# A convolution kernel generator on one Trainium2 core: twelve of W1's sixteen columns made in wide products, W2 of two channel halves in one tile

## The chip, the cores and the metric

The kernel runs on one NeuronCore of a Trainium2 chip. The core has a matrix engine (PE; PEld is its weight load), a vector engine (DVE), an activation engine (ACT), a general engine (POOL) and a queue engine for transfers (SP). The metric is the time of one execution in microseconds of device time, taken as the median of several runs.

## The reference: what is computed

```python
x   = u                                         # 1 x 2048 x 576
sa, ca, ga, sb, cb, gb = silu(c) @ w_mod        # six rows of 576
h   = layernorm(x) * (1 + ca) + sa
dt  = exp(log_dt);  A = -exp(log_A_real) + 1j * A_imag;  C = (C_real + 1j * C_imag) * dt
K   = 2 * Re( sum_n C[d,n] * exp(A[d,n] * dt[d] * l) )     # 576 channels, l = 0..2047, 128 modes
y   = causal_convolution(h, K) + h * D_skip                # by FFT
x   = x + ga * y
h   = layernorm(x) * (1 + cb) + sb
out = x + gb * (relu(h @ w1) @ w2)              # w1 576 x 4608, w2 4608 x 576
```

## The kernel before, in words

The program has two stages that matter here.

**Stage 1 (function `first`)** makes the convolution kernel K. The 128 modes lie on the partitions. Channels go in six passes, g = 0 to 5, of G = 96 channels, each as two halves (u = 0, 1) of H = 48. The position l is split as 512·s + 32·a + b: a tile W2 holds a mode's 32 values over b for each channel (complex), a tile W1 its 16 values over a, and PE multiplies them into K (`products`, 192 small matmuls a pass, bank `kps`). One pass does this:

- `exps(g+1)`: PE makes five phase banks (`ph`), ACT takes their exponential (tiles E).
- `turns(g+1)`: PE makes three phase banks, ACT rounds each to an integer (tile k), DVE subtracts it (k<-ph,k): the fraction of a turn.
- `sines(g+1)`: ACT takes sine and cosine of these; DVE and POOL multiply them with E into W2 (`half_values`); `start` makes W1's first column, through the tiles Tc and tc; `powers` makes the powers z^32, z^64 ... of each mode (tile Zp, in PSUM); DVE scales them (`moduli`).
- `doubling(g, i)`: W1's columns m to 2m are its columns 0 to m times a power, for m = 1, 2, 4, 8. Each is two products (t, T) and two sums. For m = 1, 2, 4 DVE does all four; for m = 8 POOL does the sums.
- `products(g)`: the first 96 matmuls of a pass (half u = 0) are issued after the doubling; those of u = 1, called `late`, are spread between the phase matmuls of the next pass.

The helpers `v`, `stt`, `pool`, `act` and `matmul` keep program order on each engine, so within `first` every engine's queue is the order in which the code is written. In the profile all of one helper's instructions have one line: L62 is a DVE product, sum or difference, L65 a DVE fused product, L68 one of POOL, L59 one of ACT, L71 a matmul.

**Between the stages** `conv(0)` runs in program order too: the first kernel tile gets its skip term (`skip`, kt<-kt, L1263), `h` is multiplied by ca and sa gets added (L641, L642); PE transforms the kernel tile and h (ps_f, L852), ACT evacuates them (tile Z), and DVE does butterflies over four tiles of 576 columns (`butterfly1`: W<-Z; `butterfly2`: U, K or V<-W). Beside this the last pass's products are evacuated (ke), stored to DRAM (kd), loaded back in another layout (kt) and transformed again; the product of spectra (Y, T) and the inverse transform follow.

**Stage 2 (function `ffn`)** runs four blocks of 512 rows. Each has 36 steps of matmuls into hps (L1332) and acc (L1358); the remaining convolution work (`rest`, `conv(1)` to `conv(3)`, `finish`) is cut into pieces by generators and put between them. A generator yields a number, its cost in the planner's units, and `step` draws pieces until a target is reached.

Of the kernel before, what the change touches and what calls it, by code (L numbers as in the profile page):

```python
# [49 lines left out]
class KGen:  # L50
# [22 lines left out]
    def open(self, ctx):  # L73
# [3 lines left out]
        self.ph, self.ps = pool("kg_ph", space=PSUM), pool("kg_ps", space=PSUM)  # L77

    def banks(self, name):
        return self.ph.tile([P, 2, 512], F32, tag="ph", bufs=2, name=name)  # L80

    def setup(self, I):
# [3 lines left out]
        kept = self.tc.keep_in_program_order  # L86
        tmp = lambda n: self.pw.tile([KR, NH, P], F32, tag="W2", bufs=5, name=n)
        lar, ai = tmp("lar"), tmp("ai")
        dtT = pc.tile([KR, NH], F32, name="dtT")
# [92 lines left out]
    def exps(self, g):  # L182

        E = self.E[g] = []
        for s0, n in ((0, 8), (8, 8), (16, 8), (24, 8), (32, 6)):
            e = self.pt.tile([P, 2, 8 * H], F32, tag="E", bufs=8, name=f"E_{g}")
            e = self.chunk(e, s0, n)
            self.act(e, self.times(g, self.zz[1], s0, n), AF.Exp)
            E.append(e)
            yield  # L190

    def turns(self, g):

        F = self.F[g] = []
        for s0, n in ((0, 8), (17, 8), (32, 6)):
# [17 lines left out]

    def half_values(self, g, W2, E, f, odd):


        nc, v, p = self.nc, self.v, self.pool
        j0 = 0 if odd else 16
        El, Eh = E
        su = self.chunk(self.banks(f"s_{g}"), 0, 8)  # L220
        c = None if odd else self.abs(f)
        self.act(su, f, AF.Sin, scale=TWO_PI)
        c = c if c is not None else self.abs(f)
        self.cos(c, c)
        n = 8 if odd else 7
        ends = self.start(g, su[:, :, :, 7], c[:, :, :, 7]) if odd else ()
        hi, lo = slice(j0 + 8, j0 + 16), slice(j0, j0 + n)
        for u in range(2):
            v(W2[u][:, 1, :, hi], su[:, u], Eh[:, u], ALU.mult)
            self.stt(  # L230
                W2[u][:, 1, :, lo][:, :, ::-1], su[:, u, :, 0:n], -1.0,
                El[:, u, :, 0:n][:, :, ::-1], op0=ALU.mult, op1=ALU.mult,
            )
        for u in range(2):
            p(W2[u][:, 0, :, hi], c[:, u], Eh[:, u], op=ALU.mult)
            p(
                W2[u][:, 0, :, lo][:, :, ::-1], c[:, u, :, 0:n], El[:, u, :, 0:n][:, :, ::-1],
                op=ALU.mult,
            )
            if not odd:  # L240
                nc.gpsimd.tensor_copy(W2[u][:, 0, :, 23], El[:, u, :, 7])
                nc.gpsimd.memset(W2[u][:, 1, :, 23], 0.0)
        return ends
# [18 lines left out]
    def powers(self, g, e, f):  # L262

        Z = self.ps.tile([P, 2, 512], F32, tag="Z", name=f"Zp_{g}")[:, :, 0 : 4 * G]
# [4 lines left out]
        self.act(by_u(Z[:, 1]), f[:, :, 0:4], AF.Sin, scale=-TWO_PI)  # L269
        self.act(by_u(zs[:, :, 1]), f[:, :, 4:6], AF.Sin, scale=-TWO_PI)  # L270
        self.cos(by_u(Z[:, 0]), c[:, :, 0:4])
        self.cos(by_u(zs[:, :, 0]), c[:, :, 4:6])
        for r in (1, 0):
            self.pool(by_u(zs[:, :, r]), by_u(zs[:, :, r]), e[:, :, 4:6], op=ALU.mult)
        self.Z[g] = Z, zs

        def moduli():
            for r in (1, 0):
                self.v(by_u(Z[:, r]), by_u(Z[:, r]), e[:, :, 0:4], ALU.mult)

        return moduli

    def doubling(self, g, i, u):

        v, p = self.v, self.pool
        Z = self.Z[g][0]
        m, n = 1 << i, (u.stop - u.start) * H
        W1 = self.W1[g][:, :, u].rearrange("p r u c a -> p r (u c) a")
        X, out = W1[:, :, :, 0:m], W1[:, :, :, m : 2 * m]
        zr, zi = (  # L290
            Z[:, r, i, u.start * H : u.stop * H].unsqueeze(1).unsqueeze(3)
            .broadcast_to([P, 2, n, m])
            for r in range(2)
        )
        if m == 8:
            t = self.pc.tile([P, 16 * H], F32, tag="T0", bufs=2, name="T0")
            T = self.pc.tile([P, 16 * H], F32, tag="T1", bufs=2, name="T1")
        else:
            t = self.pc.tile([P, 8 * H], F32, tag="t", bufs=2, name="t")[:, : 2 * n * m]
            T = self.ps.tile([P, 512], F32, tag="T", name="T")[:, : 2 * n * m]  # L300
        t, T = (x.rearrange("p (r c a) -> p r c a", r=2, c=n) for x in (t, T))
        v(t, X, zr, ALU.mult)
        v(T, X, zi, ALU.mult)
        yield
        add = p if m == 8 else v
        add(out[:, 0], t[:, 0], T[:, 1], op=ALU.subtract)
        add(out[:, 1], t[:, 1], T[:, 0], op=ALU.add)

# [15 lines left out]
    def first(self, setup, mod):  # L324
# [8 lines left out]
        def sines(g):  # L333
            E, F = self.E.pop(g), self.F.pop(g)
            W2 = W2s[g] = [
                self.pw.tile([P, 2, H, 32], F32, tag="W2", bufs=5, name=f"W2_{2 * g + u}")
                for u in range(2)
            ]
            ends = self.half_values(g, W2, E[2:4], F[0], True)
# [4 lines left out]
            for u in range(2):  # L344
                nc.sync.dma_start(out=k.W2d[2 * g + u], in_=W2[u].rearrange("p r c b -> p (r c b)"))
            self.moduli = self.powers(g, E[4], F[2])
# [48 lines left out]
        for g in range(NG):  # L395
            self.moduli()
            if g + 1 == NG:
                next(early)
            double = [
                self.doubling(g, i, u)  # L400
                for i, u in (
                    (0, slice(0, 2)), (1, slice(0, 2)), (2, slice(0, 1)), (2, slice(1, 2)),
                    (3, slice(0, 1)), (3, slice(1, 2)),
                )
            ]
            if g + 1 < NG:
                for i, _ in enumerate(self.exps(g + 1)):
                    some(late, 2 - i % 2)
            run(*double[:2])
            next(mod, None)  # L410
            run(double[2])
            if 0 < g < 5:
                next(early)
            if g + 1 < NG:
                turns = self.turns(g + 1)
                for _ in range(2):
                    next(turns)
                    some(late, 2)
                next(double[3])
                next(turns)  # L420
                run(late, turns, double[3])
            else:
                run(late, double[3])
# [11 lines left out]
            )  # L435
            a, late = (self.products(ps[g], self.W1[g], W2s[g][u], u) for u in range(2))
            if g + 2 == NG:
                self.kt0 = self.pw.tile([P, 16, 72], F32, tag="W2", bufs=5, name="kt_0")
                k.load_kt(self.kt0, 0, 0, nc.sync)
# [132 lines left out]
class Body:  # L572
# [34 lines left out]
    def early(self, kg):  # L607
# [23 lines left out]
        ))  # L631
        self.h0 = h = kg.pw.tile([P, 4, D], F32, tag="W2", bufs=5, name="h_0")
        for i in (0, 2, 1, 3):
# [5 lines left out]
        kept(self.skip(self.kt0, 0, nc.vector))  # L639
        for i in (0, 2, 1, 3):  # L640
            kept(nc.vector.tensor_tensor(h[:, i], h[:, i], self.m["ca"], op=ALU.mult))  # L641
            kept(nc.vector.tensor_tensor(h[:, i], h[:, i], self.m["sa"], op=ALU.add))  # L642
        self.wm = {}
        for nm in ("sb", "cb"):
            self.wm[nm] = kg.pw.tile([P, 5, D], F32, tag="W2", bufs=5, name=f"wm_{nm}")
        yield
# [14 lines left out]
    def mod(self, kg):  # L661
# [7 lines left out]
        names = (  # L669
            (2, "ga", kg.pc, "W1", 2), (1, "ca", kg.pc, "W1", 2), (0, "sa", kg.pw, "W2", 5)  # L670
        )
# [191 lines left out]
    def butterfly1(self, Z, W):  # L863
        v = self.vec.tensor_tensor
        for i in range(2):
            v(W[:, 2 * i], Z[:, i], Z[:, i + 2], op=ALU.add)
            v(W[:, 2 * i + 1], Z[:, i], Z[:, i + 2], op=ALU.subtract)
            yield 1.5

    def butterfly2(self, W, X, sgn):  # L870
# [4 lines left out]
        yield 1.5  # L875
        i, j = (1, 3) if sgn < 0 else (3, 1)
        v(X[:, i, 0], B[:, 0], Dd[:, 1], op=ALU.add)
        v(X[:, i, 1], B[:, 1], Dd[:, 0], op=ALU.subtract)
        v(X[:, j, 0], B[:, 0], Dd[:, 1], op=ALU.subtract)
        v(X[:, j, 1], B[:, 1], Dd[:, 0], op=ALU.add)  # L880
        yield 1.8

# [681 lines left out]
```

## Time and profile before

| | us |
|---|---|
| median of three runs | 1333.97 (1328.8 to 1339.76) |
| the profiled execution | 1333.12 |
| its span, first to last instruction | 1331.4 |
| mean granted PE clock | 0.945 of full |

The profile is of one execution. Its parts are a page of busy shares, a chain of what ended last (followed back from the end, each step put down to what released it), groups of equal instructions, and a list of instructions in order of time. In such a list a row has the start, the duration, the engine, the line, the operation, out<-in with shapes, the count that was merged, and in square brackets how long the engine stood idle before it and who ended that. A row of the chain has the start, the length, the engine and tile.

### The profile page before, as it was taken

The page shows a single profiled execution, that of the slowest core. Times are in us where ns is not written, and L with a number is a line of the kernel's source. Part 1 is how long each engine was busy: PE and PEld are TensorE (multiplying, and loading weights), DVE is VectorE, ACT ScalarE, POOL GpSimd, SP SyncE. Part 2 cuts the span into 40 slices and gives each one's busy share as a digit, 9 for nine tenths or more (in the row PEclk, how much of TensorE's full clock was granted, in tenths as well). Part 3 has the DMA queues.
Part 4 walks back from the last instruction along what each step waited for, and adds up shares of the span by engine and source line. Part 5 has one row for each costly group of instructions (what it writes and reads, how often), then busy time and mean ns, then how long its engine had stood idle before and what let it go on. Part 6 is the DMA issues. An engine that isn't in the chain of part 4 may idle for free.

```text
span 1331.4 us, 25993 instructions
## 1 busy us (share of the span) xinstructions
PE 1209.0 (91%) x10720; PEld 956.7 (72%) x10720; DVE 895.4 (67%) x1324; ACT 494.5 (37%) x863; POOL 162.8 (12%) x260
## 2 busy tenths in 40 slices
PE   4566676989989999999999999999999999999997
PEld 3344554667767687777777887887888888888885
DVE  5989988999986999689468993558995231111112
ACT  5678623222223422622243225433223453232321
POOL 0756502011000100100001000100000000000000
PEclk9557788999999999999999999999999999999999
DMA  8557982989878967799879985868996557666651
GB/s 272 214 221 296 304 307 84 350 296 331 307 253 304 337 224 277 247 402 342 281 276 338 357 321 156 288 203 305 346 363 198 175 181 223 198 198 202 192 168 54
DMA packets 122379, 345.85 MB, mean 260 GB/s; under 512 B 23916, under 2 KB 24212, under 8 KB 111508
## 3 DMA queue, kind: packets, MB, share of 16 engines
q1 hardware_dynamic: 105364, 226.96, 51.2%
q0 software_dynamic: 16384, 115.85, 23.1%
q8 instruction: 84, 1.38, 0.4%
q10 hardware_dynamic: 512, 1.38, 0.3%
q14 instruction: 35, 0.29, 0.1%
HBM read 262.73 MB, written 81.40 MB: 258 GB/s over the span
## 4 chain that ended last, share of the span: by engine, by line
PE 68%; DVE 17%; DMA 7%; issue 4%; ACT 2%; POOL 1%; SPq 0%; ACTq 0%; DVEq 0%; POOLq 0%
PE acc L1358 28%; PE hps L1332 27%; PE ps_f L852 5%; DMA L1d<-w 3%; PE kps L71 2%; PE ph L71 2%; DVE T L482 2%; DVE W1r L484 2%; PE ps_i L1059 2%; PE kps L517 1%; DVE w L1302 1%; DVE W1r L486 1%; DVE W1r L488 1%; DVE w L1314 1%; DVE T L62 1%
## 5 line engine op out<-in xcount | busy, mean ns | idle before, releaser
L1332 PE MATMUL hps<-xh,w 128*128 128x512 f32 x1152 | 395.2, 403 | 1.2 <-ACT xh L47 1.2
L1358 PE MATMUL acc<-w,hh 128*128 128x512 f32 x1152 | 366.4, 400 | 3.3 <-ACT hh L1337 3.2
L1338 DVE SCALAR_TENSOR_TENSOR hl<-hps,hh 128x512 fp32r<-128x512 f32 x144 | 99.0, 687 | 311.5 <-ACT hh L1337 310.8
L1332 PEld LDWEIGHTS hps<-xh,w 128*128 128x128 f32 x1152 | 217.8, 190 | 49.7 <-ACT xh L47 2.5
L1358 PEld LDWEIGHTS acc<-w,hh 128*128 128x128 f32 x1152 | 215.1, 188 | 50.6 <-ACT hh L1337 4.1
L1332 PE MATMUL hps<-xl,w 128*128 128x512 f32 x576 | 228.5, 397 | 0.7 <-DVE xl L47 0.5
L1358 PE MATMUL acc<-w,hl 128*128 128x512 f32 x576 | 223.1, 399 | 1.8 <-DVE hl L1338 1.8
L1337 ACT ACTIVATE hh<-hps 128x512 fp32r<-128x512 f32 x144 | 86.0, 597 | 327.7 <-PE hps L1332 320.5
L1307 ACT ACTIVATE w<-r 128x576 fp32r<-128x576 f32 x141 | 96.7, 686 | 216.5 <-PE acc L1358 216.1
L1332 PEld LDWEIGHTS hps<-xl,w 128*128 128x128 f32 x576 | 109.4, 190 | 24.7 <-DVE xl L47 1.7
L1358 PEld LDWEIGHTS acc<-w,hl 128*128 128x128 f32 x576 | 107.7, 189 | 26.1 <-DVE hl L1338 3.7
L1297 ACT ACTIVATE w<-r 128x640 fp32r<-128x640 f32 x140 | 102.6, 733 | 59.1 <-DMA L1d<-w 53.8
L1332 PE MATMUL hps<-xs,w 128*128 128x512 f32 x288 | 97.8, 409 | 0.0
L71 PE MATMUL kps<-W,W 128*32 128x16 f32 x2304 | 39.6, 210 | 47.3 <-POOL W L68 28.4
L1038 DVE TENSOR_TENSOR Y<-Y,T 128x1152 f32<-128x1152 f32 x60 | 79.3, 1349 | 0.0
L71 PEld LDWEIGHTS kps<-W,W 128*32 128x32 f32 x2304 | 34.8, 143 | 60.7 <-POOL W L68 31.0
L853 ACT ACTIVATE Z<-ps_f 128x288 f32<-128x288 f32 x120 | 49.0, 410 | 70.5 <-PE ps_f L852 68.5
L517 PEld LDWEIGHTS kps<-W1r,W2r 128*32 128x32 f32 x3456 | 45.2, 113 | 38.4 <-issue 19.7
L517 PE MATMUL kps<-W1r,W2r 128*32 128x48 f32 (+2 forms) x3456 | 52.5, 202 | 15.6 <-ACT ker L527 9.4
L1478 POOL DMA_DIRECT2D out_dram<-x x16 | 8.7, 545 | 466.9 <-DVE x L1470 464.5
L1332 PEld LDWEIGHTS hps<-xs,w 128*128 128x128 f32 x288 | 53.2, 188 | 11.1
L1358 PE MATMUL acc<-hh,w 128*128 128x512 f32 x144 | 57.5, 399 | 0.0
(235 smaller groups left out, 1574.5 us busy)
## 6 DMA issues: line engine op xcount, KB each, us to landing
r<-in_w_dram SPq DMA_DIRECT2D x144, 320.0 KB, 6.0
r<-in_w_dram SPq DMA_DIRECT2D x144, 288.0 KB, 3.9
w<-L1d SPq DMA_DIRECT2D x108, 320.0 KB, 4.1
w<-L2d SPq DMA_DIRECT2D x108, 288.0 KB, 2.8
W2r<-W2d POOLq DMA_DIRECT2D x18, 1536.0 KB, 9.4
W2d<-W SPq DMA_DIRECT2D x12, 1536.0 KB, 8.6
Ua<-Ud POOLq DMA_DIRECT2D x15, 1152.0 KB, 9.5
W<-W1d POOLq DMA_DIRECT2D x18, 768.0 KB, 9.6
```

Source lines behind the costliest of these rows:

```text
L71: self.tc.keep_in_program_order(self.nc.tensor.matmul(*args, **kw))
L482: v(T, X, zi, op=ALU.mult)
L517: nc.tensor.matmul(ps[32 * dd : 32 * dd + 32, q, :], W2[:, r, ch], W1[:, r, ch], start=(r == 0), stop=(r == 1),)
L852: nc.tensor.matmul(o, fc[:, n2, c, :], src(n2), start=True, stop=True)
L853: ev = nc.scalar.activation(Z[:, n2, c], ps[:, :PC], AF.Copy)
L1038: v(y, y, T, op=op or ALU.add)
L1297: copy(g - 1)(w1[g][:, 0], r1[g], AF.Copy)
L1307: copy(g)(w[:, 0:D], r2[g], AF.Copy)
L1332: nc.tensor.matmul(ps, a, x, start=(i == 0), stop=(i == 13))
L1337: nc.scalar.activation(hh, ps, AF.Relu)
L1338: nc.vector.scalar_tensor_tensor(hl, ps, 0.0, hh, op0=ALU.max, op1=ALU.subtract)
L1358: nc.tensor.matmul(acc[i], a, x, start=(f == 0 and seen[i] == 1), stop=(f == NF - 1 and seen[i] == (3 if i < 4 else 2)),)
```

## The change

Four edits:

1. The table of powers gets 384 beside 128 and 256. W1's columns 4 to 15 are made at once: columns 0 to 3 times z^128, z^256 and z^384 (`quarters`), as two products of 1152 columns for the real and two for the imaginary part on DVE, and one sum of 1152 columns each on POOL. The doublings for m = 4 and m = 8 go. Zp, the last E, the last k grow from 6 to 7 powers.
2. W2 of both halves lies in one tile (`pair`, two buffers). The sine product with the upper columns, and all of POOL's cosine products, take both halves in one instruction.
3. `h` and one weight tile share such a pair in the last pass; h is multiplied in four instructions of 1152 columns.
4. The butterflies take two tiles in one instruction (1152 columns, or 576 where there were 288), with other planner costs (1.35 for 1.5, 1.5 for 1.8).

```diff
-POWERS = (32, 64, 128, 256, 512, 1024)
+POWERS = (32, 64, 128, 256, 384, 512, 1024)
+    def pair(self, name):
+        return self.pw.tile([P, 2, 2, H, 32], F32, tag="W2", bufs=2, name=name)
...
     def half_values(self, g, W2, E, f, odd):
+        v(W2[:, :, 1, :, hi], su, Eh, ALU.mult)
         for u in range(2):
-            v(W2[u][:, 1, :, hi], su[:, u], Eh[:, u], ALU.mult)
             self.stt(
...
-        for u in range(2):
-            p(W2[u][:, 0, :, hi], c[:, u], Eh[:, u], op=ALU.mult)
...
+        p(W2[:, :, 0, :, hi], c, Eh, op=ALU.mult)
...
+    def quarters(self, g):
+        v, p = self.v, self.pool
+        W1 = self.W1[g].rearrange("p r u c a -> p r (u c) a")
+        shape = [P, G, 3, 4]
+        X = [W1[:, r, :, 0:4].unsqueeze(2).broadcast_to(shape) for r in range(2)]
+        out = [W1[:, r, :, 4:16].rearrange("p c (j a) -> p c j a", j=3) for r in range(2)]
+        zr, zi = (
+            self.Z[g][0][:, r, 2:NP].rearrange("p j c -> p c j").unsqueeze(3).broadcast_to(shape)
+            for r in range(2)
+        )
+        for r, op in ((0, ALU.subtract), (1, ALU.add)):
+            T = self.pc.tile([P, 12 * G], F32, tag="T0", bufs=2, name="T0")
+            T = T.rearrange("p (c j a) -> p c j a", j=3, a=4)
+            v(out[r], X[r], zr, ALU.mult)
+            if r:
+                yield
+            v(T, X[1 - r], zi, ALU.mult)
+            p(out[r], out[r], T, op=op)
+            yield
...
     def first(self, setup, mod):
-            run(*double[:2])
+            self.doubling(g, 0)
+            self.doubling(g, 1)
             next(mod, None)
-            run(double[2])
+            next(quarters)
...
-                next(double[3])
+                next(quarters)
                 next(turns)
-                run(late, turns, double[3])
+                run(late, quarters, turns)
...
-            run(*double[4:])
...
     def butterfly1(self, Z, W):
-        for i in range(2):
-            v(W[:, 2 * i], Z[:, i], Z[:, i + 2], op=ALU.add)
-            v(W[:, 2 * i + 1], Z[:, i], Z[:, i + 2], op=ALU.subtract)
-            yield 1.5
+        for i, op in enumerate((ALU.add, ALU.subtract)):
+            v(W[:, i::2], Z[:, 0:2], Z[:, 2:4], op=op)
+            yield 1.35
```

How this moves DVE's queue inside a pass: the rows of pass 2 from its statistics (BN_AGGR) to the first product of the next pass's sines (Tc). First before; the three k rows are the subtractions of `turns`, the T rows with 768 columns the products for m = 8, the t and T rows with 384 those for m = 4:

```order
L624 BN_AGGR mv_289<-st_1196 128x2
L62 TENSOR_TENSOR k_1200<-ph_1201,k_1200 128x768
L62 TENSOR_TENSOR t<-W_2_1041,Zp_1075 128x384
L62 TENSOR_TENSOR T<-W_2_1041,Zp_1075 128x384
L62 TENSOR_TENSOR k_1222<-ph_1223,k_1222 128x768
L62 TENSOR_TENSOR k_1248<-ph_1249,k_1248 128x2x288
L62 TENSOR_TENSOR W_2_1041<-t,T 128x48x4 x2
L62 TENSOR_TENSOR T_1257<-W_2_1041,Zp_1075 128x768
L62 TENSOR_TENSOR T_1258<-W_2_1041,Zp_1075 128x768
L62 TENSOR_TENSOR T_1263<-W_2_1041,Zp_1075 128x768
L62 TENSOR_TENSOR T_1264<-W_2_1041,Zp_1075 128x768
L62 TENSOR_TENSOR Tc<-cc,s_1370 128x192
```

And of the changed kernel, the same stretch of the same pass:

```order
L633 BN_AGGR mv_288<-st_1134 128x2
L63 TENSOR_TENSOR k_1138<-ph_1139,k_1138 128x768
L63 TENSOR_TENSOR W_2_989<-W_2_989,Zp_1015 128x96x12
L63 TENSOR_TENSOR k_1160<-ph_1161,k_1160 128x768
L63 TENSOR_TENSOR T_1181<-W_2_989,Zp_1015 128x1152
L63 TENSOR_TENSOR k_1184<-ph_1185,k_1184 128x2x336
L63 TENSOR_TENSOR Tc<-cc,s_1293 128x192
```

The third subtraction stood ahead of two sums and four products; now it stands right ahead of Tc. The first two wide products stand ahead of BN_AGGR.

On POOL, the same pass, with the semaphores each row waits for. Before: W_4 and W_5 are the two W2 tiles of the next pass, W_1 is this pass's W1 with its four sums for m = 8:

```order
L242 MEMSET W_4_1034 128x48
L241 COPY W_4_1034<-E_755 128x48 [waits Activation_49]
L68 TENSOR_TENSOR W_1_707<-T_923,T_924 128x48x8 [waits DMAHW5_49,DMAHW4_49,DVE_49]
L68 TENSOR_TENSOR W_1_707<-T_923,T_924 128x48x8
L68 TENSOR_TENSOR W_1_707<-T_929,T_930 128x48x8 [waits DVE_49]
L68 TENSOR_TENSOR W_1_707<-T_929,T_930 128x48x8
L68 TENSOR_TENSOR tc<-cc,c 128x192 [waits Activation_49,Pool_49]
```

Of the changed kernel, where W_2_983 is the next pass's pair and W_1_680 this pass's W1:

```order
L246 COPY W_2_983<-E_720 128x2x48 [waits DMAHW1_49,PE_49,DMAHW3_49,Activation_49,Pool_49]
L247 MEMSET W_2_983 128x2x48
L69 TENSOR_TENSOR W_1_680<-W_1_680,T_821 128x96x12 [waits DMAHW5_49,DMAHW4_49,DVE_49]
L69 TENSOR_TENSOR W_1_680<-W_1_680,T_872 128x96x12 [waits DVE_49]
L69 TENSOR_TENSOR tc<-cc,c 128x192 [waits Activation_49,Pool_49]
```

Two sums took the place of four, and the copy ahead of them now waits for PE and for two transfers as well: the pair was used by the pass before, whose `late` products and stores must be done.

On DVE in the last pass, from the doubling for m = 2 to the first butterfly. Before (kt is the skip term, m_gb the tile that holds it until then; t and T are buffers, numbered by use):

```order
L62 TENSOR_TENSOR W1_5_2048<-t_2110,T_2111 128x96x2 x2
L62 TENSOR_TENSOR t_2116<-W1_5_2048,Zp_5_2082 128x384
L62 TENSOR_TENSOR T_2117<-W1_5_2048,Zp_5_2082 128x384
L62 TENSOR_TENSOR W1_5_2048<-t_2116,T_2117 128x48x4 x2
L62 TENSOR_TENSOR t_2218<-W1_5_2048,Zp_5_2082 128x384
L62 TENSOR_TENSOR T_2219<-W1_5_2048,Zp_5_2082 128x384
L62 TENSOR_TENSOR W1_5_2048<-t_2218,T_2219 128x48x4 x2
L1263 TENSOR_TENSOR kt_0_1943<-kt_0_1943,m_gb_213 1x4x72
```

Of the changed kernel:

```order
L63 TENSOR_TENSOR W1_5_1921<-t_1975,T_1976 128x96x2 x2
L63 TENSOR_TENSOR W1_5_1921<-W1_5_1921,Zp_5_1947 128x96x12
L63 TENSOR_TENSOR T0_1981<-W1_5_1921,Zp_5_1947 128x1152
L63 TENSOR_TENSOR W1_5_1921<-W1_5_1921,Zp_5_1947 128x96x12
L63 TENSOR_TENSOR T0_2081<-W1_5_1921,Zp_5_1947 128x1152
L1272 TENSOR_TENSOR kt_0_1817<-kt_0_1817,m_gb_213 1x4x72
```

The skip term had only the products and sums for m = 4 ahead of it, and those for m = 8 came after h; now all four wide products stand ahead of it.

More of the change, by code (lines that the diff above doesn't have):

```diff
@@ L86, in setup @@
         kept = self.tc.keep_in_program_order
-        tmp = lambda n: self.pw.tile([KR, NH, P], F32, tag="W2", bufs=5, name=n)
-        lar, ai = tmp("lar"), tmp("ai")
+        both = self.pair("lar_ai")[:KR].rearrange("p u r c b -> p u (r c b)")
+        lar, ai = (
+            both[:, i, 0 : NH * P].rearrange("p (h n) -> p h n", n=P) for i in range(2)
+        )
         dtT = pc.tile([KR, NH], F32, name="dtT")
@@ L334, in sines @@
             E, F = self.E.pop(g), self.F.pop(g)
[L335 to L338, printed above, removed]
+            W2 = W2s[g] = self.pair(f"W2_{g}")
             ends = self.half_values(g, W2, E[2:4], F[0], True)
@@ L435, in first @@
             )
-            a, late = (self.products(ps[g], self.W1[g], W2s[g][u], u) for u in range(2))
+            a, late = (self.products(ps[g], self.W1[g], W2s[g][:, u], u) for u in range(2))
             if g + 2 == NG:
-                self.kt0 = self.pw.tile([P, 16, 72], F32, tag="W2", bufs=5, name="kt_0")
+                self.kt0 = self.pw.tile([P, 16, 72], F32, tag="WX", bufs=1, name="kt_0")
                 k.load_kt(self.kt0, 0, 0, nc.sync)
```

105 lines of the change are left out of this document (47 added, 58 removed).

## The prediction

> **What bounds the kernel now.** I read the busy time of stretches first (us; busy time and count of PE, PEld, DVE, ACT, POOL; then granted clock, DMA share, GB/s).
>
> ```profile
> 700.00:800.00 100.00, 100.00 (x436) 81.12 (x434) 91.53 (x104) 31.42 (x55) 7.57 (x13) 1.00 0.92 337
> 1000.00:1100.00 100.00, 100.00 (x452) 81.91 (x452) 39.38 (x71) 42.06 (x71) 2.18 (x4) 1.00 0.62 186
> ```
>
> In stage 2 PE is busy all the time, whether DVE works 91.5 or 39.4 us of 100: DVE time saved there, such as the wide butterflies of `conv(1)` to `conv(3)`, ends nothing earlier. What counts is when stage 2 starts. In stage 1 I first read the PE list: the rows in which `products` of passes 1 to 4 start in earnest.
>
> ```profile
> 75.42 2.22 PE L71 MATMUL kps<-W,W 128*32 128x16 f32 x148 [0.67 <-POOL W L68]
> ...
> 97.32 2.80 PE L71 MATMUL kps<-W,W 128*32 128x16 f32 x190 [0.68 <-POOL W L68]
> ...
> 115.74 2.80 PE L71 MATMUL kps<-W,W 128*32 128x16 f32 x190 [0.68 <-POOL W L68]
> ...
> 135.30 3.11 PE L71 MATMUL kps<-W,W 128*32 128x16 f32 x223 [0.67 <-POOL W L68]
> ```
>
> These passes take 21.90, 18.42 and 19.56 us; the one before, from pass 0 to 1, I take as like the first of them. Next, DVE's list of two of them: the 18.4 us pass without a wait, and the first subtraction of the 21.9 us one.
>
> ```profile
> 89.40 0.96 DVE L62 TENSOR_TENSOR k<-ph,k 128x768 f32<-128x768 f32 x1 [3.17 <-ACT k L59]
> ...
> 108.03 0.90 DVE L62 TENSOR_TENSOR k<-ph,k 128x768 f32<-128x768 f32 x1
> 108.85 0.54 DVE L62 TENSOR_TENSOR t<-W,Zp 128x384 f32<-128x384 f32 x1
> 109.31 0.55 DVE L62 TENSOR_TENSOR T<-W,Zp 128x384 f32<-128x384 f32 x1
> 109.78 1.61 DVE L62 TENSOR_TENSOR k<-ph,k 128x768 f32<-128x768 f32 x2
> 111.31 0.60 DVE L62 TENSOR_TENSOR W<-t,T 128x192 f32<-128x192 f32 x2
> 111.83 3.54 DVE L62 TENSOR_TENSOR T<-W,Zp 128x768 f32<-128x768 f32 x4
> 115.29 0.35 DVE L62 TENSOR_TENSOR Tc<-cc,s 128x192 f32<-128x192 f32 x1
> ```
>
> The fast pass is bound by DVE. The slow one is bound by a loop: POOL's sums, PE's products, the phase matmuls, ACT, DVE (3.17 us idle), POOL. So a DVE saving counts in full only in the fast pass, and there only if DVE doesn't start to wait.
>
> **What the change costs, part by part.** DVE's instructions follow each other at 0.46 us for 384 columns (108.85 to 109.31) and 0.865 for 768 (3.46 us for four, 111.83 to 115.29); so 384 more columns cost 0.405, and 1152 take 1.27. Out per pass: two m = 4 halves, each 0.93 (108.85 to 109.78) and 0.52 (111.31 to 111.83), 2.9 together, and four m = 8 products, 3.46. In: four products of 1152, 5.08. That is -1.28. The joined sine products save 2 x 0.055 = -0.11; moduli 2 x 96 columns longer, +0.2; a subtraction longer by 96, +0.1. **Net -1.1 us of DVE a pass.**
>
> But the third subtraction moves from ahead of 4 us of products to right ahead of Tc, which needs ACT's cosine. ACT's list shows the third rounding and the first cosine; an evacuation, a table load, a sine and an absolute value lie between:
>
> ```profile
> 109.61 0.65 ACT L59 ACTIVATE k<-ph 128x576 int32<-128x576 f32 x1 [1.37 <-PE ph L71]
> ...
> 113.57 0.94 ACT L59 ACTIVATE c<-c,halfpi 128x768 f32<-128x768 f32 x1
> ```
>
> The third rounding follows DVE's first subtraction (its phase matmul needs that bank), and the cosine ends at 114.51: 5.6 us after the first subtraction ends (108.93). Before, DVE had 6.36 us to do in that time (108.93 to 115.29), so nothing waited. Now it has a wide product, a subtraction, a wide product and a subtraction: 1.27 + 0.87 + 1.27 + 0.77 = 4.2. **DVE waits 1.5 us for ACT where it saved 1.1: a DVE-bound pass gets 0.4 longer, 18.8.** Queued behind the waiting Tc are the pass's sines, moduli and doublings; POOL's cosine products wait for the same cosine anyway.
>
> In a PE-bound pass the wait is free, and what counts is from the first subtraction to POOL's last sum. POOL's price for 1152 columns is not in the trace; its forms are:
>
> ```profile
> L68 POOL TENSOR_TENSOR W<-T,T 128x384 f32<-128x384 f32 x24 | 24.5, 1055 | 42.4 <-DVE T L62 35.1 <-issue 7.3
> ...
> L68 POOL TENSOR_TENSOR zs<-zs,E 128x192 f32<-128x192 f32 x12 | 7.0, 608 | 0.0
> ```
>
> By the slope from 192 to 384 (447 ns) it is 1.055 + 4 x 0.447 = 2.84; three separate ones bound it above at 3.2; a smaller slope, 2.5, below. I take 2.7, as the 192 row is of another tile. In the 21.9 us pass: first subtraction at 89.40 as before, then 0.87, 1.27, 0.87, 1.27, and the last product ends at 93.7. POOL's first sum now stands behind a copy that waits for `late` on PE, which ends where the last phase matmul starts:
>
> ```profile
> 90.64 0.79 PE ph L71 x2
> ```
>
> So sums 91.1 to 93.8 and 93.8 to 96.5; before, 97.3: **-0.8** (between -1.2 and +0.2 by the bounds). Two such passes, one of 18.8 for 18.4 and one near 18.8 for 19.6 (the DVE-bound length): `products` of pass 4 start 1.6 - 0.4 + 0.8 = 2.0 us earlier, at 133.3.
>
> Then comes the last pass and what hangs on it. Chain and DVE list:
>
> ```profile
> 140.43 0.18 DVE L628 RECIPROCAL mv<-mv 128x4 f32<-128x4 f32 x1 [0.17 <-ACT mv L626]
> ...
> 144.77 0.55 DVE L62 TENSOR_TENSOR t<-W,Zp 128x384 f32<-128x384 f32 x1
> ...
> 147.96 0.44 DVE L1263 TENSOR_TENSOR kt<-kt,m_gb 1x288 f32<-1x288 f32 x1
> ...
> 157.61 4.65 DVE L47 TENSOR_TENSOR W<-Z 128x576 f32<-128x576 f32 x4
> ...
> 165.00 2.75 DVE L47 TENSOR_TENSOR W<-Z 128x576 f32<-128x576 f32 x4
> ```
>
> The next Tc keeps its place, half a us ahead of `products` (115.29 to 115.74 before; now 5.7 and 6.2 after the first subtraction), so it is 2.0 earlier too. The reciprocal waits for ACT's root (0.17), and the root follows the sines on ACT, not DVE; as Tc now starts at its cosine and no longer 0.8 after it, the reciprocal comes later against Tc by about 0.7: 2.0 - 0.7 = 1.3 earlier than before. Between it and the skip term stood 3.19 us of m = 4 (144.77 to 147.96); now four wide products, 5.1: +1.9. **The skip term comes 0.6 later.** From there the chain of waits runs through PE's transforms, the last products, two transfers of the kernel tile and its second transform to the butterfly of the last row:
>
> ```profile
> 148.61 13.37 PE ps_f L852 x48
> ...
> 163.73 6.02 issue
> ...
> 195.99 0.23 DVE K L47
> ```
>
> All of it moves by +0.6. The joined h products (8 of 576 at 0.67 by the slope to 4 x 1.27, -0.3) and the three wide butterflies from 157 on (2 x 1.27 and 4 x 0.67 is 5.2 each, where 6 x 0.67 and 4 x 0.36 is 5.5 and the first lost 1.9 more, 4.65 to 2.75) are hidden by it; without that cover they would give 0.3 + 0.9 + 1.9 = 3.1. That a first wide butterfly needs all eight evacuations and not four is hidden likewise. After 195.99 one and a half butterflies save 0.4. Stage 2 starts 0.2 later, and **1333.1 + 0.2 = 1333.3**; the median shown is 0.85 above its profiled run, so I say 1334.
>
> **A rule against it.** When POOL's sums of the last pass ran beside butterflies, four W<-Z took 4.65 us (157.61) and alone 2.75 (165.00). The Trainium skill, SBUF — State Buffer, section "Who interferes with whom", says that a DVE instruction with two SBUF inputs and a GpSimd instruction that reads SBUF contend for one shared port pair, an exclusive lock. The trace agrees that they slow each other. Now the skip term, with two such inputs, follows the last product just as the first wide sum ends and the second starts; caught behind one, it and all after it come up to 2.7 us later.
>
> **Rivals.**
> - *The saving comes through* (0.2): ACT is ready earlier than I think, or the chain at 148 isn't what counts. Five passes of -1.1, +1.9 at the skip term and -0.4: 1329. With DVE the bound to the end, the sixth pass's -1.3 and the hidden 3.1 in place of the +1.9: -10.3, 1323. Say 1327. For it: no DVE wait in the pass at 108. Against: the 5.6 us.
> - *The wide products run slower than contiguous ones* (0.1, the other side). Their columns come in runs of four, three powers apart in PSUM. The t row of m = 1, runs of one, took 0.477, where 0.55 for 384 (109.31) less 0.20 would be 0.35:
>
> ```profile
> L62 DVE TENSOR_TENSOR t<-W,Zp 128x192 f32<-128x192 f32 x6 | 2.9, 477 | 0.2
> ```
>
>   127 ns per 192 is 0.76 per wide product. Two of four are off the path in each pass (under the wait, or under PE), two on it: 5 x 1.52 + 4 x 0.76 = 10.6, so 1344. It decides from about 1.4 us a product. Against: rows with runs of two and four (0.46 for 384) show no such price.
> - *POOL becomes the bound* (0.1): sums of 3.7, a sixth over my upper bound, make three passes +1.2 in place of -0.8 (90.64 + 0.5 + 7.4 is 98.5), +6; or the skip term is caught, +2.7. 1336 to 1342, say 1340.
> - *The pauses without a releaser on PE* (6.02 at 163.73, and smaller) shift (0.1): plus or minus 5.
>
> **How the numbers follow.** Forecast 0.5, 1329 to 1339, predicted time 1334. The range 1325 to 1342 takes in most of the first rival and of the third. About 1% (13 us) is what a measurement of this kernel tells from no change: faster by more needs all savings and a lost pause, 0.04; slower by more needs the slow products and a second mishap, 0.06; the rest 0.9.
>
> **What would show it.** In the changed profile: wide products of 1.27 to 1.35 us; Tc idle 1 to 2 us for ACT's cosine in each pass; `products` of pass 4 at 132 to 135; skip term at 147 to 150; stage 2's first hps row at 223 to 228. I am wrong if Tc starts without a wait, if POOL's sums exceed 3.2 us, or if stage 2 starts outside those bounds.

## The result, and the profile after

| | before | after |
|---|---|---|
| median of seven runs, us | 1329.86 (1328.67 to 1339.76) | 1344.68 (1340.73 to 1350.7) |
| the profiled execution | 1333.12 | 1342.17 |
| its span | 1331.4 | 1340.3 |
| mean granted PE clock | 0.945 | 0.94 |

The ratio on record, to which this document keeps, is 1.0085 with a 95% interval of 1.0061 to 1.0110 (the two medians alone would give 1.011): the changed kernel is slower by 0.85%. That is inside "within 1%", where the prediction had put 0.9. But the forecast was no change (1334), and 1344.68 lies 2.7 us above the range's upper end.

Where did the time go? ACT makes one `hh` in each of the 144 steps of stage 2, so these rows serve as milestones. Each kernel's list at step 22, in block 0, and at the last step, first before, then after:

```profile
432.67 0.59 ACT L1337 ACTIVATE hh<-hps 128x512 fp32r<-128x512 f32 x1
...
1314.29 0.60 ACT L1337 ACTIVATE hh<-hps 128x512 fp32r<-128x512 f32 x1 [5.75 <-PE hps L1332]
```

```profile
432.65 0.59 ACT L1346 ACTIVATE hh<-hps 128x512 fp32r<-128x512 f32 x1
...
1323.24 0.60 ACT L1346 ACTIVATE hh<-hps 128x512 fp32r<-128x512 f32 x1 [5.75 <-PE hps L1341]
```

At step 22 the two kernels are level, after all of stage 1. All 9 us are lost behind it, in the stage that the prediction called covered. By the same rows the lateness is 5.82 at step 42, 7.68 at step 90 and 8.95 at the last; what follows accounts for the 5.8 up to step 42. The busy times of four stretches of the changed kernel (columns as in the prediction) show where PE stopped being busy:

```profile
455.00:500.00 45.00, 42.06 (x177) 32.38 (x176) 43.45 (x51) 14.61 (x26) 3.19 (x6) 0.99 0.70 247
500.00:545.00 45.00, 39.58 (x160) 30.30 (x160) 42.41 (x71) 11.02 (x20) 1.05 (x2) 0.97 0.69 243
700.00:800.00 100.00, 100.00 (x434) 80.70 (x433) 87.31 (x87) 31.60 (x56) 8.08 (x14) 1.00 0.94 350
1000.00:1100.00 100.00, 100.00 (x448) 81.62 (x447) 40.54 (x63) 39.15 (x65) 0.00 (x0) 1.00 0.63 185
```

And two of them before:

```profile
455.00:500.00 45.00, 44.71 (x192) 35.02 (x192) 43.86 (x63) 15.18 (x27) 3.30 (x7) 1.00 0.76 260
500.00:545.00 45.00, 41.93 (x174) 32.72 (x173) 41.30 (x73) 14.19 (x27) 0.95 (x2) 0.96 0.78 277
```

The stretches at 700 and 1000, the only ones that the prediction read, are as full as they were. From 455 to 545 PE was not always busy before either (86.64 of 90 us), and there it loses 5.0 more. DVE is busy for 43 of 45 us: it is the bound here. The chain of waits of before had said so, in three of its pieces:

```profile
469.24 2.54 DVE T L1036 x2
471.78 2.54 DVE Y L1038 x2
...
500.42 10.30 DMA Ua<-Ud
```

What DVE waits for stands in its list. Before, `conv(1)` forms K from the tiles Z. Half of its `butterfly1` starts at 430.72, half of a later `butterfly1` at 450.69, and then comes the product with Ua, which POOL has loaded from DRAM:

```profile
430.72 0.74 DVE L866 TENSOR_TENSOR W<-Z 128x576 f32<-128x576 f32 x1
...
450.69 0.76 DVE L866 TENSOR_TENSOR W<-Z 128x576 f32<-128x576 f32 x1
451.36 0.75 DVE L867 TENSOR_TENSOR W<-Z 128x576 f32<-128x576 f32 x1
...
453.50 2.62 DVE L1036 TENSOR_TENSOR T<-K,Ua 128x1152 f32<-128x1152 f32 x2
```

After:

```profile
435.45 2.63 DVE L876 TENSOR_TENSOR W<-Z 128x1152 f32<-128x1152 f32 x2 [0.73 <-ACT Z L863]
...
456.55 1.36 DVE L1045 TENSOR_TENSOR T<-K,Ua 128x1152 f32<-128x1152 f32 x1 [4.44 <-DMA Ua<-Ud]
457.83 2.62 DVE L876 TENSOR_TENSOR W<-Z 128x1152 f32<-128x1152 f32 x2
```

Three things changed. The first wide butterfly starts at 435.45, when ACT has evacuated the last Z, where half of it ran at 430.72. So K is saved 1.0 us later and the load of Ua issued 0.7 later (POOL's list, before and after):

```profile
440.01 0.55 POOL L843 DMA_DIRECT2D Rd<-K  x1 [3.54 <-DVE K L880]
...
446.06 0.54 POOL L839 DMA_DIRECT2D Ua<-Ud  x1 [2.85 <-DMA Rd<-K]
```

```profile
441.05 0.55 POOL L853 DMA_DIRECT2D Rd<-K  x1 [4.61 <-DVE K L889]
...
446.73 0.53 POOL L849 DMA_DIRECT2D Ua<-Ud  x1 [2.35 <-DMA Rd<-K]
```

The load itself took longer, too: 9.8 us from issue to landing, where it took 7.4 before. That is the larger part of Ua's lateness, and why it did is not shown. And the half butterfly that filled DVE's time until Ua landed (450.69) is now part of a wide one, which needs Z tiles that are not there yet (ACT starts on the last at 455.23) and stands behind the product with Ua (457.83). DVE idles 4.44 us, and there is no slack behind it. PE then waits for what DVE makes:

```profile
488.44 1.21 PE L1068 MATMUL ps_i<-V,gc 128*128 128x288 f32 x4 [1.04 <-DVE V L882]
...
497.28 1.24 PE L1068 MATMUL ps_i<-V,gc 128*128 128x288 f32 x4 [1.20 <-DVE x L1073]
```

In stage 1, the rows in which `products` of passes 1 to 4 start, and the transform behind the skip term, from PE's list of after:

```profile
75.01 2.21 PE L72 MATMUL kps<-W,W 128*32 128x16 f32 x148 [2.31 <-POOL W L69]
...
95.98 2.80 PE L72 MATMUL kps<-W,W 128*32 128x16 f32 x190 [2.30 <-POOL W L69]
...
115.87 2.80 PE L72 MATMUL kps<-W,W 128*32 128x16 f32 x190 [2.31 <-POOL W L69]
...
135.22 3.23 PE L72 MATMUL kps<-W,W 128*32 128x16 f32 x225 [2.33 <-POOL W L69]
...
151.53 5.64 PE L862 MATMUL ps_f<-kt,fcK 128*128 128x288 f32 x16 [5.33 <-issue]
```

Pass 4 comes 0.08 us earlier (135.30 before), not 2.0. The transform comes 2.9 us later (148.61 before). By the first hps row 0.94 of that is left (225.76 for 224.82), and by step 22 nothing.

### The profile page after: what moved, and what is told of

It is laid out like the page before. It is cut to its first block, busy times and chain, and to the rows that moved or that the text cites. A ratio compares the mean times of both kernels' runs of the same rounds, so it can differ in the third digit from the quotient of the medians.

```text
span 1340.3 us, 25783 instructions
## 1 busy us (share of the span) xinstructions
PE 1216.0 (91%) x10720; PEld 960.2 (72%) x10720; DVE 882.2 (66%) x1168; ACT 497.9 (37%) x863; POOL 166.8 (12%) x212
## 4 chain that ended last, share of the span: by engine, by line
PE 64%; DVE 18%; DMA 9%; issue 5%; ACT 2%; POOL 2%; SPq 0%; POOLq 0%; ACTq 0%; DVEq 0%
PE hps L1341 25%; PE acc L1367 24%; PE ps_f L862 4%; DMA Ua<-Ud 4%; PE kps L526 3%; DVE T L1045 3%; DVE Y L1047 3%; PE kps L72 2%; DMA L1d<-w 2%; PE ph L72 2%; DVE W L876 1%; POOL W L69 1%; PE ps_i L1068 1%; DMA r<-in_w_dram 1%; DVE T L491 1%
```

## The experiments

All ratios are to the kernel before on the same chip. Lateness is against the profile before, at step 0, 22, 42 and the last step; each is of one execution, so its start in stage 2 is good to a few us only (the runs of one kernel spread over some 10 us). The last column, what a kernel loses from step 22 to 42, is what separates them. What is lost after step 42 does not: 3.1 us in the changed kernel, but also 2.0 in e1, 3.5 in e9 and 0.0 in e11, all with the old butterflies; its cause stays open.

| kernel | ratio | 95% | late at 0 | 22 | 42 | end | 22 to 42 |
|---|---|---|---|---|---|---|---|
| changed | 1.0085 | 1.0061 to 1.0110 | 0.95 | -0.02 | 5.82 | 8.95 | 5.8 |
| e1, old butterflies | 1.0039 | 1.0021 to 1.0057 | 2.04 | -1.57 | -1.12 | 0.84 | 0.4 |
| e2, edit 4 alone | 1.0070 | 1.0045 to 1.0095 | 0.96 | -1.09 | 5.23 | 9.91 | 6.3 |
| e3, wide, old costs | 1.0061 | 1.0040 to 1.0082 | 1.68 | 1.32 | 4.79 | 6.03 | 3.5 |
| e4, first butterfly in halves | 1.0053 | 1.0034 to 1.0071 | 5.47 | 4.18 | 3.64 | 5.10 | -0.5 |
| e5, skip term first | 1.0026 | 1.0006 to 1.0047 | 6.38 | 6.13 | 5.75 | 6.15 | -0.4 |
| e6, sums early | 0.9994 | 0.9969 to 1.0018 | 4.32 | 3.62 | 3.23 | 6.65 | -0.4 |
| e7, edit 1 alone | 1.0000 | 0.9979 to 1.0022 | -0.54 | -0.69 | -0.83 | 1.35 | -0.1 |
| e8, new costs alone | 1.0011 | 0.9989 to 1.0033 | 4.87 | 2.29 | 5.71 | 7.91 | 3.4 |
| e9, stores by POOL | 1.0008 | 0.9991 to 1.0025 | -0.91 | -2.48 | -2.69 | 0.85 | -0.2 |
| e10, products at once | 1.0079 | 1.0054 to 1.0104 | 11.01 | 9.96 | 9.57 | 11.68 | -0.4 |
| e11, edits 2 and 3 alone | 1.0004 | 0.9990 to 1.0019 | 1.83 | 0.28 | 0.28 | 0.32 | 0.0 |
| e12, all orders | 1.0008 | 0.9988 to 1.0029 | -0.45 | -2.01 | -2.46 | -0.84 | -0.4 |

### The butterflies: e1 to e4, and e8

**e1** is the changed kernel with the butterflies and costs of before.

```diff
-        for i, op in enumerate((ALU.add, ALU.subtract)):
-            v(W[:, i::2], Z[:, 0:2], Z[:, 2:4], op=op)
-            yield 1.35
+        for i in range(2):
+            v(W[:, 2 * i], Z[:, i], Z[:, i + 2], op=ALU.add)
+            v(W[:, 2 * i + 1], Z[:, i], Z[:, i + 2], op=ALU.subtract)
+            yield 1.5
```

> The changed kernel with the old butterflies: two tiles a yield, 576 and 288 columns, old planner costs. Edits 1 to 3 stay. Theory A (the wide butterflies cost the time, in stage 2, since a wide one starts only when all eight evacuations are there, and DVE has no slack between 430 and 540 us): level with before, 1327 to 1335, and the lateness of stage 2's steps against before is under 1.5 us after step 42, where the changed kernel has 5.8. Theory B (the new stage 1 shifts the transfers, and the loss in stage 2 follows from that): as the changed kernel, 1340 to 1346.

It measured 1.0039 and loses 0.4 us from step 22 to 42 where the changed kernel loses 5.8. **e2** is the counterpart, the kernel before with edit 4 alone:

```diff
-            v(W[:, 2 * i], Z[:, i], Z[:, i + 2], op=ALU.add)
-            v(W[:, 2 * i + 1], Z[:, i], Z[:, i + 2], op=ALU.subtract)
-            yield 1.5
+            v(W[:, i::2], Z[:, 0:2], Z[:, 2:4], op=op)
+            yield 1.35
...
-        yield 1.8
+        yield 1.5
```

> The kernel before with only the wide butterflies and their new planner costs (edit 4 alone). Theory A: slower by about 8 us, 1336 to 1342, with PE waiting for DVE near 490 to 530 us. Theory B: level with before or up to 3 us faster, since stage 1 is as before.

1.0070: most of the loss, with stage 1's code untouched. DVE's list has the wait for Ua:

```profile
456.23 1.36 DVE L1035 TENSOR_TENSOR T<-K,Ua 128x1152 f32<-128x1152 f32 x1 [5.18 <-DMA Ua<-Ud]
```

Edit 4 has two parts. **e3** keeps the wide instructions and gives the planner the old costs:

```diff
-            yield 1.35
+            yield 1.5
...
-        yield 1.5
+        yield 1.8
```

> The changed kernel with the wide butterflies, but the planner's costs of before (1.5 and 1.8 in place of 1.35 and 1.5). Theory A1 (the form costs the time: its start waits for all eight evacuations): no change against the changed kernel, 1340 to 1346. Theory A2 (the lower costs cost it, because the planner puts more work into a step than DVE can do): most of the 9 us come back, 1329 to 1336.

It measured 1.0061 and loses 3.5 us from step 22 to 42. **e8** is the kernel before with the new costs and no other change:

```diff
-            yield 1.5
+            yield 1.35
...
-        yield 1.8
+        yield 1.5
```

> The kernel before with only the planner's costs of the butterflies lowered (1.35 and 1.5 for 1.5 and 1.8), the instructions as before. By the traces of the changed kernel, e2 and e3, stage 2 loses 8 to 9 us with wide butterflies and new costs, 4.3 with wide butterflies and old costs. Theory A1 (the form is what costs, through the late start): at most 2 us slower, 1330 to 1334. Theory A2 (the costs alone shift work and PE waits for DVE): 4 us slower or more, 1335 to 1339.

Its trace loses 3.4 us in the same place, as PE's busy time from 500 on shows (41.93 before):

```profile
500.00:545.00 45.00, 40.11 (x159) 30.62 (x158) 42.25 (x75) 10.77 (x20) 1.05 (x2) 0.92 0.69 243
```

There the lower costs put more products ahead of what PE needs from DVE: a weight tile w starts at 520.95, behind four T and Y instructions in a row from 515.87 on, and PE waits for it as it does not before:

```profile
521.22 0.79 PE L1358 MATMUL acc<-hh,w 128*128 128x512 f32 x1 [1.31 <-DVE w L1313]
```

The changed kernel waits 1.98 us at the same row (521.21); e3, with the old costs, has no such wait and loses its time earlier, at 489 to 499 us. The time of e8, 1.0011, is not told apart from no change. **e4** has the first butterfly in halves, the second wide, and the old cost for the first:

```diff
-        for i, op in enumerate((ALU.add, ALU.subtract)):
-            v(W[:, i::2], Z[:, 0:2], Z[:, 2:4], op=op)
-            yield 1.35
+        for i in range(2):
+            v(W[:, 2 * i], Z[:, i], Z[:, i + 2], op=ALU.add)
+            v(W[:, 2 * i + 1], Z[:, i], Z[:, i + 2], op=ALU.subtract)
+            yield 1.5
```

> The changed kernel with the first half of each butterfly in the old form (two tiles a yield at 1.5, so that it starts on four evacuations), and the second half in the wide form at 1.5. Theory A1: level with before, 1327 to 1335, and K's butterfly in block 0 starts near 431 us as before and not at 435. Theory A2 or a fault in the second half's form: as the changed kernel, 1339 to 1346.

Its busy time and DVE list:

```profile
455.00:500.00 45.00, 45.00 (x194) 35.21 (x194) 44.28 (x58) 15.62 (x29) 3.20 (x6) 1.00 0.78 277
```

```profile
454.87 0.76 DVE L876 TENSOR_TENSOR W<-Z 128x576 f32<-128x576 f32 x1 [0.18 <-ACT Z L863]
455.54 0.75 DVE L877 TENSOR_TENSOR W<-Z 128x576 f32<-128x576 f32 x1
...
458.11 1.36 DVE L1046 TENSOR_TENSOR T<-K,Ua 128x1152 f32<-128x1152 f32 x1 [0.35 <-DMA Ua<-Ud]
```

The half butterfly stands in DVE's wait again, PE is busy for all 45 us, and nothing is lost from step 22 to 42. So by the traces, one execution of each, the wide first butterfly costs 3.5 us there, the new costs 3.4, both together 5.8 (with edits 1 to 3) and 6.3 (without), and each of the eight kernels without either is within 0.5 of before. The wait for Ua is 4.4 to 5.2 us in the three kernels with a wide first butterfly, and 0 to 2.2 in the ten others and in the kernel before; the load of Ua takes 9.8 to 10.5 us in those three and 7.4 to 9.5 in the rest.

By the times, edit 4 is certain (e2; and the changed kernel over e1, 0.46% with intervals of 0.2 each). Its parts one by one are not: e3 over e1 is 0.22% and e8 0.11%, both inside their intervals. Nor do the times show what e4 should gain over e3 (1.0053 and 1.0061); in its one profile it entered stage 2 already 5.5 us late, and whether that is its stage 1 or that execution stays open.

### Edits 1 to 3: e7, e11, e9

e1 left 0.39% with edits 1 to 3. **e7** is the kernel before with edit 1 alone, the powers and `quarters`:

```diff
-POWERS = (32, 64, 128, 256, 512, 1024)
+POWERS = (32, 64, 128, 256, 384, 512, 1024)
...
-            run(double[2])
+            next(quarters)
```

> The kernel before with edit 1 alone: the three powers and the wide products; W2 stays in separate tiles, h in four single rows, butterflies old. Theory C: edit 1 carries the cost of edits 1 to 3, so 1335 to 1339, with the ps_f row 16 us after the products of pass 4. Rival E (the joined tile costs it, since POOL's copy and ACT's h now wait for PE's late products and for transfers): level with before, 1329 to 1334.

**e11** has edits 2 and 3 alone, the pair:

```diff
+    def pair(self, name):
+        return self.pw.tile([P, 2, 2, H, 32], F32, tag="W2", bufs=2, name=name)
```

> The kernel before with edits 2 and 3 alone: W2 of both halves in one tile, h and a weight tile in such a pair, butterflies and doublings as before. The order of SP's queue here has the last stores of W2 ahead of the load of sb's weights. Theory F: level with before, 1329 to 1334. Rival G: 3 to 6 us slower, 1335 to 1339.

They measured 1.0000 and 1.0004: neither has a cost by itself that these runs can tell. Together they cost 0.39% (interval 0.21 to 0.57; the two alone could reach its lower end). One thing that appears only together stands in SP's queue of the last pass. Before:

```profile
143.49 2.43 SPq L345 DMA_DIRECT2D W2d<-W  x2
```

After:

```profile
146.26 0.39 SPq L731 DMA_DIRECT2D h_sb<-in_w_mod_dram  x1
146.75 0.92 SPq L360 DMA_DIRECT2D W2d<-W  x2
```

The load of a weight tile into h's half of the pair now stands ahead of the two stores of W2. It waits until the `late` products have read the pair (the last end at 146.20), and the stores, behind it, start 3.3 us later than before, although POOL's last product into their tile has ended at 142.84. In e11 they still stand ahead of that load (145.06 and 148.42). **e9** is e1 with these two stores issued by POOL:

```diff
-                nc.sync.dma_start(out=k.W2d[2 * g + u], in_=W2[:, u].rearrange("p r c b -> p (r c b)"))
+                (nc.gpsimd if g + 1 == NG else nc.sync).dma_start(out=k.W2d[2 * g + u], in_=W2[:, u].rearrange("p r c b -> p (r c b)"))
```

> As e1 (edits 1 to 3, old butterflies), but the two stores of the last pass's pair (W2d, 1.5 MB each) are issued by POOL's queue instead of SP's. In e1 and the changed kernel SP's queue has the load of sb's weights into h's pair ahead of these stores; it waits for the late products of pass 4 until 146 us, and the stores start at 146.7 where they started at 143.5 before. Theory F (this wait is what edits 2 and 3 cost: transfers left idle at 140 to 146 collide later with the last products and the kernel tile): stores issued at 142 to 144, time level with before, 1330 to 1335. Rival G (the joined tile costs through its other waits, POOL's copy and ACT's h): as e1, 1335 to 1339.

POOL issues them when its last product is done:

```profile
143.32 1.12 POOL L360 DMA_DIRECT2D W2d<-W  x2 [0.30 <-POOL W L69]
```

The ratio falls from 1.0039 to 1.0008 (intervals of 0.0018 and 0.0017 to each side, on two chips): a fall of 0.31%, with some 0.25 to each side. How the later stores reach the end is seen only in part: the transfers move 175 and 327 GB/s in the two stretches of 10 us from 136 on after, 169 and 306 in e1, 230 and 359 in e9, 241 and 346 before. But e11 has 178 and 364 and loses nothing, so this alone does not settle it.

### The order in stage 1: e5, e6, e10, e12

The skip term came 2.9 us later since four wide products stand ahead of it. **e5** is e1 with the skip term moved right behind the doubling for m = 2, and h between the products:

```diff
+            if g + 1 == NG:
+                run(late)
+                next(early)
             next(quarters)
-            if 0 < g < 5:
+            if g > 0:
                 next(early)
...
-            if g + 1 == NG:
-                next(early)
```

> The changed kernel with the old butterflies (as e1), and in the last pass the skip term right after the doubling for m = 2, then the first two wide products, h, and the last two. Theory C (edits 1 to 3 cost their 5 us by the skip term, which stands behind four wide products): the first ps_f row comes 11 to 12 us after the products of pass 4, where all four runs with the changed stage 1 have 16.3 and the two with the old one 13.3; the time is 3 to 5 us below e1, 1330 to 1334, level with before. Rival D (that lateness is given back before stage 2, since the transfers of the kernel tile set its start): as e1, 1335 to 1339.

The first transform came 4.8 us sooner after `products` than in e1, and the time fell by 0.13% only, less than its interval. e7 says the same from the other side: its first transform comes 16.3 us after `products` (136.07 to 152.37), as late as in e1, and its time is level with before. So the late skip term is not by itself what edits 1 to 3 cost. The chain shows what is late next: the second transform of the kernel tile now stands behind PE's products for the modulation.

```profile
189.14 3.78 PE mps_gb L743 x48
192.92 1.26 PE ps_f L903 x2
```

**e6** adds to e5 that both imaginary wide products stand ahead of the second subtraction, and that POOL's copy and memset stay where the code has them:

```diff
                 next(quarters)
+                next(quarters)
                 next(turns)
```

> As e5, and in passes 0 to 4 both wide products of the imaginary part directly follow the first subtraction, and POOL's copy into the next pair stands behind its products with the cosine, not ahead of the wide sums. Theory C extended (each pass is the loop POOL's sums, PE's products and phases, ACT, DVE; the copy waits for PE's late products and holds both sums back): each pass 1 us shorter, the products of pass 4 start at 130 to 132 instead of 135 to 137, and the time is 3 to 5 us below e5, 1326 to 1331. Rival: the passes are bound by DVE or ACT, or stage 2 gives it back: as e5.

0.9994: level with before, and 0.32% below e5, about the size of their joint interval. The mechanism behind the expectation did not come: `products` of pass 4 start at 134.22, not at 130 to 132, and the passes still take 20.2 to 20.5 us. e6 still has the stores behind the load, so that load is not the only thing that can be mended. **e10** is e7 with all four wide products right behind the doubling for m = 2 (and the skip term first, as in e5):

```diff
-            next(quarters)
+            run(quarters)
...
-                next(quarters)
                 next(turns)
-                run(late, quarters, turns)
+                run(late, turns)
```

> Edit 1 alone on the kernel before (as e7), with all four wide products and both sums directly behind the doubling for m = 2 in every pass, and in the last pass the skip term first, h between the second and the third product. If the single effects add (e1 to e6 took 0.45% off, e7 stands at 0), 0.3 to 0.6% faster than before: 1324 to 1329. Rival: ACT's chain of roundings, sines and exponentials (20 us a pass without a pause longer than 0.8) sets the passes, and the last products and weights set the end, so that nothing is gained: 1330 to 1335.

1.0079, the worst order in stage 1. DVE's first subtraction now stands behind two more products, PE's third phase matmul waits for it, and ACT's third rounding for PE. A row of PE's list and one of ACT's:

```profile
115.47 0.93 PE L72 MATMUL ph<-dp,zt 112*128 112x336 f32 x2 [1.47 <-DVE k L63]
```

```profile
116.50 0.73 ACT L60 ACTIVATE k<-ph 128x672 int32<-128x672 f32 x1 [2.24 <-PE ph L72]
```

`products` start at 52.73, 74.33, 96.02, 117.71 and 139.39: 21.7 us a pass. **e12** is e6 with the last pass's stores by POOL, e9's line:

```diff
-                nc.sync.dma_start(
+                (nc.gpsimd if g + 1 == NG else nc.sync).dma_start(
```

> Edits 1 to 3 with old butterflies and the three reorderings together: the skip term first in the last pass (e5), the wide products of the imaginary part ahead of the second subtraction and POOL's copy behind its cosine products (e6), and the last pair's stores issued by POOL (e9). If the effects add (e1 at +0.39%; e5 took 0.13 of it, e6 a further 0.32, e9 by itself 0.31), 0.2 to 0.5% faster than before: 1326 to 1330. Rival: e6 and e9 give the same microseconds, those of transfers that start earlier, and what is left is set by ACT's 20 us a pass: level with before, 1330 to 1335.

1.0008, level with before again: the two remedies do not add up. The line that took 0.31% off e1 takes nothing off e6, so the order in SP's queue is not shown to be the cost of edits 1 to 3; what that cost is made of stays open. No version is faster than the kernel before.

## Why the prediction was right or wrong, point by point

**That butterflies in stage 2 are hidden** failed, and it is the main error. The step was "PE is busy all the time ... DVE time saved there ends nothing earlier", read from two stretches, 700 to 800 and 1000 to 1100, and from it "that a first wide butterfly needs all eight evacuations and not four is hidden likewise". The sentence holds where it was read. From 455 to 545, where the butterflies of `conv(1)` stand, DVE bound the kernel before, too. The wide form saved DVE time there (2.63 for two of 1152, 2.75 for four of 576) and lost more by starting later and by leaving DVE nothing to do in a longer wait for Ua. The costs (1.35 and 1.5) were not priced at all: e8 shows that they move the planner's pieces, and 3.4 us in its trace. None of the three signs by which the prediction would have known itself wrong looks behind the start of stage 2. That the result still fell "within 1%" is luck: the sum behind it had no term for what was lost.

**Durations** held. A wide product on DVE starts 1.26 after the one before (109.53 to 110.79; predicted 1.27), so the rival of slow products is out, though its 1344 is, by chance, what came. POOL's two sums take 5.22, 2.61 each (predicted 2.7, bounds 2.5 and 3.2). DVE's list, a row of ACT's and one of POOL's, of the pass from 95.98:

```profile
108.66 0.96 DVE L63 TENSOR_TENSOR k<-ph,k 128x768 f32<-128x768 f32 x1 [0.40 <-ACT k L60]
109.53 1.34 DVE L63 TENSOR_TENSOR W<-W,Zp 128x1152 f32<-128x1152 f32 x1
110.79 0.95 DVE L63 TENSOR_TENSOR k<-ph,k 128x768 f32<-128x768 f32 x1
...
114.13 0.36 DVE L63 TENSOR_TENSOR Tc<-cc,s 128x192 f32<-128x192 f32 x1 [0.36 <-ACT s L60]
```

```profile
113.28 0.81 ACT L60 ACTIVATE s<-k 128x768 f32<-128x768 f32 x1
```

```profile
110.59 5.22 POOL L69 TENSOR_TENSOR W<-W,T 128x1152 f32<-128x1152 f32 x2
```

**Tc idle 1 to 2 us for the cosine** failed: it waits 0.36, for the sine, which ends at 114.09. The prediction misread its own row: Tc<-cc,s reads the sine s, and the cosine goes to tc on POOL. (Its 5.6 less 4.2 is also 1.4, not 1.5.) So a wait of 1.5 us stood in the sum that the kernel does not have. The saving on DVE is real, and Tc comes 5.5 us after the first subtraction where it came 7.3 after it.

**Products of pass 4 at 133.3** failed (135.22). The two slow passes went as forecast: pass 2 starts its products 1.34 us earlier (95.98), where 1.6 was predicted. The term that failed is the length of a DVE-bound pass, 18.4 and then 18.8. In the changed kernel two passes take 19.89 and 19.35, and their chain runs over ACT's roundings, POOL's sums (to 115.8) and `products` at 115.87. POOL's copy, which the prediction had put ahead of the sums in the slow passes only, holds them back here as well: the first sum's last input is ready at 107.29, and it starts at 110.59. That the 18.4 us pass was bound by DVE was read from one execution, in which the clock was high just there. Busy times of before, and of e2, whose stage 1 has the same code:

```profile
100.00:120.00 20.00, 11.96 (x441) 8.88 (x435) 19.73 (x44) 17.72 (x25) 15.23 (x21) 0.76 0.80 307
```

```profile
100.00:120.00 20.00, 14.38 (x402) 10.46 (x402) 18.71 (x41) 16.22 (x24) 13.98 (x20) 0.51 0.74 284
```

With a granted clock of 0.51 in place of 0.76 PE is busy 2.4 us longer in 20, and the pass takes 19.7 (e8, with the same code again: 0.57 and 19.5). Which of the two leads is not shown. But a pass that DVE alone bounds is the exception, and the saving of DVE lies beside ACT, PE and POOL in the others.

**The skip term** was right in its parts and wrong in its sum. The four products for the m = 4 work added 1.9, as predicted; the reciprocal came 1.1 later against `products` (predicted 0.7); the -2.0 ahead of them did not come. That is +2.9 for +0.6: 150.85, past the bounds of 147 to 150. **Stage 2's start** was inside its bounds (225.76), +0.94 for +0.2, but not by the prediction's path, on which all of the skip term's lateness passes on: of 2.9 us only 0.94 arrived.

**The rule against the change** did not decide. The Trainium skill, SBUF — State Buffer, section "Who interferes with whom", has a DVE instruction with two SBUF inputs and a GpSimd one that reads SBUF shut each other out. The last pass shows the two holding each other up, in DVE's and POOL's lists:

```profile
150.85 0.57 DVE L1272 TENSOR_TENSOR kt<-kt,m_gb 1x288 f32<-1x288 f32 x1
151.36 1.34 DVE L654 TENSOR_TENSOR h_sb<-h_sb,m_ca 128x1152 f32<-128x1152 f32 x1
152.73 3.70 DVE L654 TENSOR_TENSOR h_sb<-h_sb,m_sa 128x1152 f32<-128x1152 f32 x1
...
157.73 1.36 DVE L654 TENSOR_TENSOR h_sb<-h_sb,m_sa 128x1152 f32<-128x1152 f32 x1
```

```profile
148.50 6.71 POOL L69 TENSOR_TENSOR W<-W,T 128x1152 f32<-128x1152 f32 x2 [3.48 <-DVE T L63]
```

Of the two instructions on h beside the second sum the first keeps its 1.34, and the second takes 3.70 where the same one takes 1.36 alone: it ends at 156.43, 1.2 us after the sums (155.21). POOL's sums take 6.71 for 5.22. The skip term itself slipped through (0.57), and what was caught, h, came behind it.

**What the prediction did not have** is SP's queue: it followed the copy on POOL that now waits for the pair, and not the load into the pair that stands ahead of the stores. That e9 takes most of e1's 0.39% away is measured; by which way is seen only in part, and that the same line takes nothing off e6 speaks against the queue as the only cause.

## What to carry to other kernels

Before you call work in a long stage hidden, read the bound in the stretch in which that work stands, not in the stage's fullest stretches; the chain of waits of the kernel before named DVE there. A wider instruction saves its overhead and starts only when its last input is there: where an engine takes its work in the order of the code, as DVE here, its narrow halves also fill waits that the wide one must stand behind. And where a tile gets a new tenant, follow every transfer that now waits for it, with what is queued behind it.

## What the runs showed that was not expected

- The granted clock of one stretch of stage 1 differs between executions of the same code (0.76 and 0.51 from 100 to 120), and a pass with it (18.4 and 19.7 us). One profile of such a stretch says little on a term of a microsecond.
- One of DVE's 1152-column instructions with two SBUF inputs took 2.7 times as long beside POOL's sum (3.70 for 1.36), while the wide products, whose power is read from PSUM, kept 1.26 from start to start. What an instruction loses beside POOL differs between executions of the same code: one of four columns (L629) took 4.81 us beside POOL's products with the cosine in e8 and 1.04 before. That is 3.8 us of one profile, where e8 was 4.87 late at step 0.
- A planner's cost lowered by 0.15 and 0.3 moved 3.4 us in a trace without any instruction changing; the times do not tell the kernel from before.
